# One-token attention with a gated MLP: where q is picked, how many key blocks TensorE scores, and the order of the last two tiles

## The chip, the cores and the metric

The kernel runs on one core of a Trainium2 chip. A core has a matrix engine (TensorE, PE in the profile), a vector engine (VectorE, DVE), a scalar engine (ScalarE, ACT), a general engine (GpSimd, POOL), and SyncE (SP), which here only issues DMA transfers. Sixteen DMA engines carry the transfers. The engines run side by side, each with its own list of instructions in order, and wait for each other by semaphores. The metric is the device time of one execution in microseconds (us); smaller is better.

## The reference

A gate mixes two branches that read the same token `x` of 512 values (everything is bfloat16):

```python
g = sigmoid((x * gate_w).sum(-1))
q = (x @ wq)                         # 32 heads of 128
scores = einsum("bhqd,bhkd->bhqk", q, k) * 128 ** -0.5    # 4096 keys per head
a = einsum("bhqk,bhkd->bhqd", softmax(scores), v) @ wo    # back to 512
h = relu(x @ w1 + b1)                # 1376 units
b = (h * h) @ w2 + b2
out = g * a + (1 - g) * b
```

The caches `k` and `v` have 32 heads x 4096 keys x 128 values, 33.5 MB each; `wq` and `wo` have 4.2 MB each, `w1` and `w2` 1.4 MB each. Each head has its own keys and values, and there is one query row, so every cached value is used once.

## The kernel before

**Tiles.** The attention goes over `NQ = 8` tiles of four heads. A tile of K is 128 partitions x 128 blocks x 128 values: partition `p` holds 128 consecutive keys of head `p // 32`, and a "block" is one key of every partition. A tile of K or V is one transfer of 4.19 MB. Three buffers hold K and two hold V; the last two V tiles are put in K's buffers.

**Scores in three ways.** The 128 blocks of a tile are divided:

- GpSimd multiplies four groups of `GB[i]` blocks by q (L308, into two buffers `pg`); VectorE sums each group over the 128 values (`psums`, L680).
- VectorE multiplies two groups of `XH[i]` blocks by q (`prods`, L665, q read from PSUM as `pQ`) and sums them (`sums`, L674).
- TensorE takes the rest in `NC[i]` chunks of eight blocks: it transposes each block (`transposes`, L428), ScalarE copies a chunk out of PSUM (`evac`, L336), and TensorE multiplies it by q (`scores`, L442); ScalarE copies the scores to `Sb` (`score_copy`, L342).

Before the change `NC` is 4 for tiles 0 to 2 and 5 after; `GB` and `XH` follow as 17 and 14, or 16 and 12.

**Softmax and values.** VectorE takes the maximum of each partition (`smax`, L687); TensorE transposes it (`max_rows`, L452), VectorE takes the maximum per head (`gmax`, L691), TensorE sends it back to all partitions (`max_cols`, L456), ScalarE negates it (`neg_max`, L346) and does the exponentials (`exps`, L353). TensorE multiplies them with V (`pv`, L473), ScalarE copies the result to `pvf` (`pv_copy`, L359), and TensorE adds the four useful rows into `O` (`extract`, L482). This is done for tile `i-1` and `i-2` while the scores of tile `i` are made.

**The start.** TensorE makes a column form of `x`, which ScalarE copies to `xcol` and, spread over 128 columns, to `xb`. Then it multiplies `xb` by `wq` for one tile after the other (L413). Each result has q of four heads in four diagonal pieces, which are picked into `qb`: even tiles by ScalarE (L328), odd tiles by VectorE (L652). Three PSUM buffers `T` hold the results, so a result waits until the one three before was picked. Semaphores `s_qb` and `s_qd` count the picked pieces of the two engines.

**The MLP.** Its hidden row is made on TensorE after tile 0's scores (`mlp_h`), copied by ScalarE, turned into columns `H` (`mlp_c`), and VectorE makes `(1 - g) * relu(h) ** 2` as `hs` in six operations, three shapes of two each (`mlp`, L698 and L701). `mlp_out` multiplies by `w2`. All MLP weights lie in the third K buffer, so K of tile 2 is loaded only after `mlp_out` (`s_ml`, L248). VectorE makes `b2g = (1 - g) * b2` in tile 1 (L725).

**The order of the transfers.** SyncE issues nearly all of them, in a fixed order (L269 to L292): K 0, MLP weights, `b2`, the last rows of `w2` in eight small transfers, K 1, V 0, K 2, then V and K in turn, and `wo` in five parts by rows (`TS`). A K load waits until its buffer was read by TensorE, VectorE and GpSimd (`s_t`, `s_mu`, `s_pm`), a V load until the product with the tile two before is done (`s_pv`).

**The end.** After the last tile, VectorE scales `O` (L732) and TensorE regroups it into columns `o2` (L545). `attn_rows` goes over the parts of `wo` as they land: rows up to 20 as wide products into `pO` (L555), which ScalarE copies to `pvf` (L383) and `wide_rows` adds to `acc` (L570); the others straight into `acc` (L561). VectorE adds `b2g` (L737) and SyncE stores the result.

The order on TensorE and VectorE at the end of the last loop is written out by hand. For VectorE, inside the loop over tiles:

```python
psums(i, 1)
prods(i, 1)
if i + 1 < NQ:
    q_psum(i + 1)
if i == 0:
    mlp()
if i == 1:
    eng.wait_ge(s_bb, 16)
    eng.tensor_scalar(b2g[:, :], b2w[:, :], omg[:, 0:1], None, ALU.mult).then_inc(s_g, 1)
psums(i, 2)
sums(i, 1)
```

Of the kernel before, what the change touches and what calls it, by code (L numbers as in the profile page):

```python
# [5 lines left out]
def bass_gated_mix__gqa_block_cached__dense_activation_squared_relu__decode_kernel(  # L6
# [30 lines left out]
    FG = 9  # L37
# [14 lines left out]
    NC = [4 if i < 3 else 5 for i in range(NQ)]  # L52
# [18 lines left out]
    TS = [0, 8, 16, 24, 30, 32]  # L71
# [15 lines left out]
    with ctx:  # L87
# [88 lines left out]

        s_x = sem("s_x")
# [60 lines left out]
        with nc.Block() as block:  # L238

            @block.sync  # L240
            def _(eng):
# [33 lines left out]
                eng.dma_start(b2w[0:128:32, :], B_b2.rearrange("(j p) -> j p", p=128)).then_inc(s_bb, 16)  # L275
# [18 lines left out]
            @block.gpsimd  # L294
            def _(eng):
                eng.memset(ident[:, :], 0.0).then_inc(s_id, 1)
                eng.wait_ge(s_id, 1)
                eng.affine_select(out=ident[:, :], in_=ident[:, :], compare_op=ALU.not_equal, fill=1.0,
                                  base=0, pattern=[[-1, 128]], channel_multiplier=1).then_inc(s_id, 1)
                for i in range(NQ):  # L300
                    eng.wait_ge(s_k[i % NK], 16 * (i // NK + 1))
                    eng.wait_ge(s_qd if i % 2 else s_qb, 4 * (i // 2 + 1))
                    g = GB[i]
                    for k in range(GP):
                        n = GP * i + k
                        if n >= 2:
                            eng.wait_ge(s_ps, n - 1)
                        eng.tensor_tensor(pg[:, n % 2, 0:g, :], Kt[:, i % NK, k * g * 128:(k + 1) * g * 128]  # L308
                                          .rearrange("p (b d) -> p b d", b=g),
                                          qb[:, i:i + 1, :].broadcast_to([128, g, 128]), ALU.mult)\  # L310
                           .then_inc(s_pm, 1)

            @block.scalar
            def _(eng):
                eng.dma_start(xrow[:, :], A_x[0, :, :]).then_inc(s_x, 16)
                eng.dma_start(grow[:, :], gate_w.rearrange("(a n) -> a n", a=1)).then_inc(s_x, 16)
                eng.dma_start(b1r[:, :], B_b1.rearrange("(a n) -> a n", a=1)).then_inc(s_b, 16)
                eng.wait_ge(s_xc, 1)
                eng.activation(xcol[:, :], XC, ACT.Copy).then_inc(s_xf, 1)
# [4 lines left out]
                for j in range(0, NQ, 2):  # L324
                    eng.wait_ge(s_qr, j + 1)
                    for h in range(4):
                        a, b = HP * h, HP * h + HP
                        eng.activation(qb[a:b, j, :], T[j % NT][a:b, h * 128:(h + 1) * 128], ACT.Copy)\  # L328
                           .then_inc(s_qb, 1)
# [31 lines left out]
                for i in range(NQ + 1):  # L361
                    if i == NQ:
                        pv_copy(NQ - 3)
                    if i < NQ:
# [15 lines left out]
                pv_copy(NQ - 2)  # L380
                pv_copy(NQ - 1)
                eng.wait_ge(s_ww, 1)
                eng.activation(pvf[:, :], pO[0:112, :], ACT.Copy).then_inc(s_wc, 1)  # L383

            @block.tensor
            def _(eng):
# [8 lines left out]
                eng.wait_ge(s_xf, 2)  # L395
                eng.wait_ge(s_zp, 1)
                eng.matmul(Z, onesf[:, :], zp[:, :], start=True, stop=True).then_inc(s_z, 1)

                def q_wait(j):
                    eng.wait_ge(s_qd if j % 2 else s_qb, 4 * (j // 2 + 1))  # L400

                def q_columns(j):
                    q_wait(j)
# [3 lines left out]
                eng.wait_ge(s_xf, 2)  # L407
                eng.wait_ge(s_wq, 16)
                for j in range(NQ):
                    if j >= NT:  # L410
                        q_wait(j - NT)
# [106 lines left out]
                def mlp_x():  # L518
                    eng.wait_ge(s_hs, 3)
# [53 lines left out]
                for i in range(NQ):  # L573
# [21 lines left out]
                    if i >= 2:  # L595
                        pv(i - 2, NG // 2, NG)
                max_rows(NQ - 1)
                extract(NQ - 3)
                max_cols(NQ - 1)
                pv(NQ - 2, 0, NG)  # L600
# [12 lines left out]
            def _(eng):  # L613
# [11 lines left out]
                for p, q in ((0, 0), (32, 20)):  # L625
# [10 lines left out]
                                         ALU.add, zp[:, :]).then_inc(s_zp, 1)  # L636
                eng.wait_ge(s_ez, 1)
# [5 lines left out]
                eng.wait_ge(s_g, 3)  # L643
                def q_psum(i):
                    eng.wait_ge(s_qd if i % 2 else s_qb, 4 * (i // 2 + 1))
                    eng.tensor_copy(PQ[:, i % 4, :], qb[:, i, :]).then_inc(s_pq, 1)

                for j in range(1, NQ, 2):
# [45 lines left out]
                def mlp():  # L694
                    eng.wait_ge(s_h, 2)
                    parts = [(128, 0, FG), (FR, FG, FN), (QX, FN, FN + TX)]
                    for p, a, b in parts:
                        eng.tensor_scalar(hr[0:p, a:b], H[0:p, a:b], 0.0, None, ALU.max).then_inc(s_hv, 1)  # L698
                    eng.wait_ge(s_hv, 3)
                    for p, a, b in parts:  # L700
                        eng.scalar_tensor_tensor(out=hs[0:p, a:b], in0=hr[0:p, a:b], scalar=omg[0:p, 0:1],  # L701
                                                 in1=hr[0:p, a:b], op0=ALU.mult, op1=ALU.mult)\
                           .then_inc(s_hs, 1)

                for i in range(NQ + 1):
# [10 lines left out]
                    if i < NQ:  # L716
                        psums(i, 1)
                        prods(i, 1)
                        if i + 1 < NQ:
                            q_psum(i + 1)  # L720
                        if i == 0:
                            mlp()
                        if i == 1:
                            eng.wait_ge(s_bb, 16)
                            eng.tensor_scalar(b2g[:, :], b2w[:, :], omg[:, 0:1], None, ALU.mult).then_inc(s_g, 1)  # L725
                        psums(i, 2)
                        sums(i, 1)
                eng.wait_ge(s_den, 1)
                eng.reciprocal(rden[:, :], DEN).then_inc(s_rd, 1)
                eng.wait_ge(s_rd, 1)  # L730
# [3 lines left out]
                eng.tensor_copy(o2[:, :], T[1][:, 0:NH]).then_inc(s_o2, 1)  # L734
                eng.wait_ge(s_acc, 1)
# [31 lines left out]
```

## Time and profile before

| | us |
|---|---|
| three runs, median (lowest to highest) | 191.07 (190.68 to 191.09) |
| the profiled execution: time | 191.85 |
| its span | 189.6 |
| VectorE busy | 150.3 |
| GpSimd busy | 132.9 |
| TensorE products busy | 105.0 |
| ScalarE busy | 74.5 |
| bytes moved by DMA | 78.47 MB, mean 414 GB/s |

The profile shows one execution. Its span runs from the first to the last instruction; the device time has some 2.3 us more around it. All times below are from the start of the span. A row of a group gives the line, the engine, the operation, the tiles (written <- read) with their shapes, the count, the busy time and the mean of one. A row of a timeline has start, duration, and the instruction. A row of a window has the length, then busy time and count for PE, PE's weight loads, DVE, ACT and POOL, then the granted TensorE clock, the busy share of the 16 DMA engines and GB/s.

### The profile page before, as it was taken

Reading aid. Unit: us, or ns where it says so; the run is one execution under the profiler, and the core shown is the slowest. Engines: PE = TensorE matmul, PEld = TensorE weight load, DVE = VectorE, ACT = ScalarE, POOL = GpSimd, SP = SyncE. Lnnn points to the kernel's source line nnn. Section 1 sums busy time; section 2 is a strip of 40 time slices with the busy share of each in tenths; the row PEclk is TensorE's granted clock in tenths of the full one; section 3 lists DMA queues with packets and bytes.
Section 4 is the critical chain, followed back from the end, with each engine's and each line's share of the span. In section 5 each row is a group of like instructions: output and inputs, shape, how many; then the busy total and the mean of one; then the engine's idle time right before and its main releaser. Section 6 shows DMA issues by size and latency. Waiting matters only on the chain. (4 is left out here: it accounts for less than half of the span.)

```text
span 189.6 us, 2722 instructions
## 1 busy us (share of the span) xinstructions
PE 105.0 (55%) x1118; PEld 61.7 (33%) x1118; DVE 150.3 (79%) x134; ACT 74.5 (39%) x174; POOL 132.9 (70%) x38
## 2 busy tenths in 40 slices
PE   1129867748212705942952775396284767139755
PEld 0113343307112701631541444235141752023512
DVE  6102489699999999999999999999999999960010
ACT  2103464208240800880295078139505571405201
POOL 1000199949699459998999999999999999900000
PEclk9999998857655555695695588559657675855965
DMA  6999899999999999999999999999999999999991
GB/s 221 443 442 442 381 441 412 429 442 442 439 430 423 415 429 422 436 432 436 442 432 436 429 404 429 436 429 436 432 442 436 436 404 436 418 430 398 418 411 64
DMA packets 3841, 78.47 MB, mean 414 GB/s; under 512 B 484, under 2 KB 590, under 8 KB 887
## 3 DMA queue, kind: packets, MB, share of 16 engines
q1 hardware_dynamic: 3824, 78.32, 97.0%
q8 instruction: 8, 0.13, 0.3%
q14 instruction: 3, 0.02, 0.0%
q10 hardware_dynamic: 6, 0.00, 0.0%
HBM read 78.32 MB, written 0.00 MB: 413 GB/s over the span
## 5 line engine op out<-in xcount | busy, mean ns | idle before, releaser
L308 POOL TENSOR_TENSOR pg<-Kt,qb 128x2048 f32<-128x2048 bf16 (+1 forms) x32 | 132.2, 4160 | 32.6 <-DMA Kt<-in_A_k_cache_dram 21.4
L680 DVE TENSOR_REDUCE Sb<-pg 128x16 f32<-128x2048 f32 (+1 forms) x32 | 74.3, 2323 | 0.1
L336 ACT ACTIVATE kT<-T 128x1024 bf16<-128x1024 bf16 x37 | 35.3, 1034 | 9.2 <-PE T L428 9.0
L428 PE MATMUL T<-ident,Kt 128*128 128x128 bf16 x296 | 24.8, 249 | 10.5 <-DMA Kt<-in_A_k_cache_dram 10.5
L665 DVE TENSOR_TENSOR pr<-Kt,pQ 128x1536 f32<-128x1536 bf16 (+1 forms) x16 | 29.5, 1844 | 1.0
L674 DVE TENSOR_REDUCE Sb<-pr 128x12 f32<-128x1536 f32 (+1 forms) x16 | 29.4, 1838 | 0.0
L428 PEld LDWEIGHTS T<-ident,Kt 128*128 128x128 bf16 x296 | 21.2, 113 | 14.0 <-DMA Kt<-in_A_k_cache_dram 11.9
L346 ACT ACTIVATE nM<-pM 128x4 f32<-128x4 f32 x8 | 1.4, 173 | 57.8 <-PE pM L456 57.8
L473 PE MATMUL pO<-Vt,E 128*16 128x512 bf16 x192 | 22.9, 568 | 1.0 <-issue 1.0
L442 PE MATMUL pS<-qc,kT 128*128 128x4 bf16 x296 | 13.3, 167 | 14.4 <-ACT kT L336 14.0
L353 ACT ACTIVATE E<-Sb,nM 32x128 bf16<-32x128 f32 x32 | 18.7, 584 | 0.9
L452 PE MATMUL pM<-identf,mp 128*1 128x128 f32 x8 | 3.0, 372 | 28.5 <-DVE mp L687 28.5
L442 PEld LDWEIGHTS pS<-qc,kT 128*128 128x128 bf16 x296 | 10.6, 100 | 18.3 <-ACT kT L336 18.1
L482 PE MATMUL pX<-pvf,pick 112*32 112x128 f32 x64 | 13.6, 385 | 1.4 <-ACT pvf L359 1.4
L652 DVE CAST qb<-T 32x128 bf16<-32x128 f32 x16 | 4.6, 287 | 10.2 <-PE T L413 9.8
L413 PE MATMUL T<-Vt,kT 128*128 128x512 bf16 x32 | 10.2, 462 | 3.5 <-DMA Vt<-in_A_wq_dram 3.5
L482 PEld LDWEIGHTS pX<-pvf,pick 112*32 112x32 f32 x64 | 9.1, 153 | 5.4 <-ACT pvf L359 2.8
L452 PEld LDWEIGHTS pM<-identf,mp 128*1 128x1 f32 x8 | 0.6, 80 | 29.8 <-DVE mp L687 29.8
L473 PEld LDWEIGHTS pO<-Vt,E 128*16 128x16 bf16 x192 | 6.6, 108 | 7.9 <-issue 6.4
L456 PE MATMUL pM<-gm,onesf 1*128 1x4 f32 x16 | 4.5, 349 | 6.8 <-DVE gm L691 6.3
L328 ACT ACTIVATE qb<-T 32x128 bf16<-32x128 f32 x16 | 4.3, 268 | 10.0 <-PE T L413 9.7
L353 ACT ACTIVATION_READ_ACCUMULATOR E<-Sb,nM 32x1 f32 x32 | 8.2, 255 | 0.0
(81 smaller groups left out, 74.6 us busy)
## 6 DMA issues: line engine op xcount, KB each, us to landing
Kt<-in_A_k_cache_dram SPq DMA_DIRECT2D x8, 4096.0 KB, 27.3
Vt<-in_A_v_cache_dram SPq DMA_DIRECT2D x6, 4096.0 KB, 28.5
Vt<-in_A_wq_dram SPq DMA_DIRECT2D x1, 4096.0 KB, 12.4
Kt<-in_A_v_cache_dram SPq DMA_DIRECT2D x1, 4096.0 KB, 33.8
Kt<-in_A_v_cache_dram SPq DMA_DIRECT2D x1, 3072.0 KB, 24.7
Vt<-in_A_wo_dram SPq DMA_DIRECT2D x3, 1024.0 KB, 30.9
Kt<-in_B_w_dram SPq DMA_DIRECT2D x1, 1376.0 KB, 24.5
Kt<-in_B_w_dram SPq DMA_DIRECT2D x1, 1152.0 KB
```

The lines of the kernel that those rows point to most:

```text
L308: eng.tensor_tensor(pg[:, n % 2, 0:g, :], Kt[:, i % NK, k * g * 128:(k + 1) * g * 128] .rearrange("p (b d) -> p b d", b=g), qb[:, i:i + 1, ...
L336: eng.activation(kT[:, n % NR, :], T[n % NT][:, :].bitcast(bf16), ACT.Copy).then_inc(s_ev, 1)
L353: eng.activation(E[a:b, j % NE, :, h], Sb[a:b, j % NS, :], ACT.Exp, bias=nM[a:b, 4 * j + h:4 * j + h + 1], scale=SCALE, accum_out=RS[a:b, ...
L413: mm = eng.matmul(T[j % NT][:, :], xb[:, t, :], wq_sb[:, t, j * 512:(j + 1) * 512], start=(t == 0), stop=(t == 3))
L428: mm = eng.transpose(T[n % NT][:, :].bitcast(bf16)[:, y * 128:(y + 1) * 128], Kt[:, i % NK, w * 128:(w + 1) * 128], ident[:, :])
L442: mm = eng.matmul(S[:, c * TC + y, :], kT[:, n % NR, y * 128:(y + 1) * 128], qc[:, 4 * i:4 * i + 4], start=True, stop=True)
L473: mm = eng.matmul(pO[r:r + 16, :], E[:, i % NE, 4 * y:4 * y + 4, :], VT(i)[:, y * 512:(y + 1) * 512], start=(y < 4), stop=(y >= NG - 4))
L482: mm = eng.matmul(O, pick[0:112, b, 28 - 4 * i:60 - 4 * i], pvf[:, b * 128:(b + 1) * 128], start=False, stop=(i == NQ - 1 and b == 3), ski ...
L652: eng.tensor_copy(qb[a:b, j, :], T[j % NT][a:b, h * 128:(h + 1) * 128]).then_inc(s_qd, 1)
L665: eng.tensor_tensor(pr[:, 0:x, :], Kt[:, i % NK, a * 128:(a + x) * 128] .rearrange("p (b d) -> p b d", b=x), PQ[:, i % 4:i % 4 + 1, :].bro ...
L674: eng.tensor_reduce(Sb[:, i % NS, a:a + x], pr[:, 0:x, :], AX.X, ALU.add).then_inc(s_sd, 1)
L680: eng.tensor_reduce(Sb[:, i % NS, k * g:(k + 1) * g], pg[:, n % 2, 0:g, :], AX.X, ALU.add)\
```

## The change

- All tiles have `NC = 4`: 32 blocks on TensorE, four groups of 17 on GpSimd, two groups of 14 on VectorE.
- q of tiles 1, 3 and 5 is picked by VectorE, of tiles 0, 2, 4, 6 and 7 by ScalarE.
- `mlp` is two operations over the whole of `H`, placed after VectorE's third sums of GpSimd's products.
- `b2g` is made at the start, before q is picked; the transfer of `b2` goes from SyncE's queue to ScalarE's.
- `xcol` is copied by VectorE.
- TensorE does the extraction of tile 5 and the product of tile 6 with V ahead of the last tile's maximum; ScalarE copies the result of tile 6 ahead of the last negated maximum. VectorE does the copy of tile 7's result and the one after the wide products.
- `wo` comes in four parts: the first two are joined.

```diff
-    NC = [4 if i < 3 else 5 for i in range(NQ)]
+    NC = [4] * NQ
...
-    TS = [0, 8, 16, 24, 30, 32]
+    TS = [0, 16, 24, 30, 32]
...
+        QD = [1, 3, 5]
+        QA = [j for j in range(NQ) if j not in QD]
+
+        def wait_q(eng, j):
+            if j in QD:
+                eng.wait_ge(s_qd, 4 * (QD.index(j) + 1))
+            else:
+                eng.wait_ge(s_qb, 4 * (QA.index(j) + 1))
...
                 eng.wait_ge(s_wm, 2)
-                eng.dma_start(b2w[0:128:32, :], B_b2.rearrange("(j p) -> j p", p=128)).then_inc(s_bb, 16)
...
                 eng.dma_start(b1r[:, :], B_b1.rearrange("(a n) -> a n", a=1)).then_inc(s_b, 16)
+                eng.wait_ge(s_wm, 1)
+                eng.dma_start(b2w[0:128:32, :], B_b2.rearrange("(j p) -> j p", p=128)).then_inc(s_bb, 16)
                 eng.wait_ge(s_xc, 1)
-                eng.activation(xcol[:, :], XC, ACT.Copy).then_inc(s_xf, 1)
...
-                for j in range(0, NQ, 2):
+                for j in QA:
...
                     if i == NQ:
                         pv_copy(NQ - 3)
+                        pv_copy(NQ - 2)
...
-                pv_copy(NQ - 2)
-                pv_copy(NQ - 1)
-                eng.wait_ge(s_ww, 1)
-                eng.activation(pvf[:, :], pO[0:112, :], ACT.Copy).then_inc(s_wc, 1)
...
-                max_rows(NQ - 1)
                 extract(NQ - 3)
-                max_cols(NQ - 1)
                 pv(NQ - 2, 0, NG)
+                max_rows(NQ - 1)
+                max_cols(NQ - 1)
                 extract(NQ - 2)
...
+                eng.wait_ge(s_xc, 1)
+                eng.wait_ge(s_xf, 1)
+                eng.tensor_copy(xcol[:, :], XC).then_inc(s_zp, 1)
...
+                eng.wait_ge(s_bb, 16)
+                eng.tensor_scalar(b2g[:, :], b2w[:, :], omg[:, 0:1], None, ALU.mult).then_inc(s_g, 1)
...
-                for j in range(1, NQ, 2):
+                for j in QD:
...
-                    parts = [(128, 0, FG), (FR, FG, FN), (QX, FN, FN + TX)]
-                    for p, a, b in parts:
-                        eng.tensor_scalar(hr[0:p, a:b], H[0:p, a:b], 0.0, None, ALU.max).then_inc(s_hv, 1)
-                    eng.wait_ge(s_hv, 3)
-                    for p, a, b in parts:
-                        eng.scalar_tensor_tensor(out=hs[0:p, a:b], in0=hr[0:p, a:b], scalar=omg[0:p, 0:1],
-                                                 in1=hr[0:p, a:b], op0=ALU.mult, op1=ALU.mult)\
-                           .then_inc(s_hs, 1)
+                    eng.tensor_scalar(hr[:, :], H, 0.0, omg[:, 0:1], ALU.max, ALU.mult).then_inc(s_hv, 1)
+                    eng.wait_ge(s_hv, 1)
+                    eng.scalar_tensor_tensor(out=hs[:, :], in0=H, scalar=0.0, in1=hr[:, :], op0=ALU.max, op1=ALU.mult)\
+                       .then_inc(s_hs, 1)
...
+                        psums(i, 2)
                         if i == 0:
                             mlp()
-                        if i == 1:
-                            eng.wait_ge(s_bb, 16)
-                            eng.tensor_scalar(b2g[:, :], b2w[:, :], omg[:, 0:1], None, ALU.mult).then_inc(s_g, 1)
-                        psums(i, 2)
                         sums(i, 1)
...
+                eng.wait_ge(s_pv, NQ)
+                eng.tensor_copy(pvf[:, :], pO[0:112, :]).then_inc(s_pc, 1)
                 eng.wait_ge(s_rd, 1)
...
+                eng.wait_ge(s_ww, 1)
+                eng.tensor_copy(pvf[:, :], pO[0:112, :]).then_inc(s_wc, 1)
                 eng.wait_ge(s_acc, 1)
```

More of the change, by code (lines that the diff above doesn't have):

```diff
@@ L301, in _ @@
                     eng.wait_ge(s_k[i % NK], 16 * (i // NK + 1))
-                    eng.wait_ge(s_qd if i % 2 else s_qb, 4 * (i // 2 + 1))
+                    wait_q(eng, i)
                     g = GB[i]
@@ L394, in _ @@
                 mm.then_inc(s_xc, 1)
-                eng.wait_ge(s_xf, 2)
-                eng.wait_ge(s_zp, 1)
+                eng.wait_ge(s_xf, 1)
+                eng.wait_ge(s_zp, 2)
                 eng.matmul(Z, onesf[:, :], zp[:, :], start=True, stop=True).then_inc(s_z, 1)
-                def q_wait(j):
-                    eng.wait_ge(s_qd if j % 2 else s_qb, 4 * (j // 2 + 1))
                 def q_columns(j):
-                    q_wait(j)
+                    wait_q(eng, j)
                     eng.transpose(QT[:, j, :], qb[:, j, :], ident[:, :]).then_inc(s_qt, 1)
-                eng.wait_ge(s_xf, 2)
                 eng.wait_ge(s_wq, 16)
@@ L410, in _ @@
                     if j >= NT:
-                        q_wait(j - NT)
+                        wait_q(eng, j - NT)
                     for t in range(4):
@@ L518, in mlp_x @@
                 def mlp_x():
-                    eng.wait_ge(s_hs, 3)
+                    eng.wait_ge(s_hs, 1)
                     eng.matmul(HX, selh[:, :], hs[0:QX, FN:FN + TX], start=True, stop=True).then_inc(s_hx, 1)
@@ L596, in _ @@
                         pv(i - 2, NG // 2, NG)
+                extract(NQ - 3)
+                pv(NQ - 2, 0, NG)
                 max_rows(NQ - 1)
-                extract(NQ - 3)
                 max_cols(NQ - 1)
-                pv(NQ - 2, 0, NG)
                 extract(NQ - 2)
@@ L636, in _ @@
                                          ALU.add, zp[:, :]).then_inc(s_zp, 1)
+                eng.wait_ge(s_xc, 1)
+                eng.wait_ge(s_xf, 1)
+                eng.tensor_copy(xcol[:, :], XC).then_inc(s_zp, 1)
                 eng.wait_ge(s_ez, 1)
@@ L643, in _ @@
                 eng.wait_ge(s_g, 3)
+                eng.wait_ge(s_bb, 16)
+                eng.tensor_scalar(b2g[:, :], b2w[:, :], omg[:, 0:1], None, ALU.mult).then_inc(s_g, 1)
                 def q_psum(i):
-                    eng.wait_ge(s_qd if i % 2 else s_qb, 4 * (i // 2 + 1))
+                    wait_q(eng, i)
                     eng.tensor_copy(PQ[:, i % 4, :], qb[:, i, :]).then_inc(s_pq, 1)
-                for j in range(1, NQ, 2):
+                for j in QD:
                     eng.wait_ge(s_qr, j + 1)
```

## The prediction

> **What bounds the kernel now.** I read the forty slices and the queues first. No slice of the DMA row between the first and the last is below 8, so I then asked for the stretches as windows.
>
> ```profile
> DMA  6999899999999999999999999999999999999991
> q1 hardware_dynamic: 3824, 78.32, 97.0%
> q8 instruction: 8, 0.13, 0.3%
> ```
>
> ```profile
> 32.00:172.00 140.00, 76.12 (x840) 48.33 (x842) 133.74 (x91) 59.26 (x135) 123.07 (x30) 0.66 1.00 430
> 172.00:184.00 12.00, 9.10 (x102) 4.13 (x94) 0.74 (x3) 3.52 (x10) 0.00 (x0) 0.78 0.98 408
> 184.00:187.20 3.20, 2.27 (x56) 1.13 (x60) 0.00 (x0) 0.60 (x1) 0.00 (x0) 0.50 0.48 193
> ```
>
> The last two columns are the busy share of the 16 DMA engines and GB/s: 1.00 and 430 for 140 us. VectorE is busy 133.74 us in the same stretch, but the transfers never stop for it. The third line has a share of 0.48: the engines do not finish together. The trace's landing records put the sixteen completions of the last wo transfer between 184.94 and 187.11, mean 186.07; the slowest engine sets the time. That last landing is also the issue of the fifth wo transfer (152.71) plus its time to landing:
>
> ```profile
> Vt<-in_A_wo_dram SPq DMA_DIRECT2D x1, 256.0 KB, 34.4
> ```
>
> The chain that ended last says the same, and adds a second thread beside it:
>
> ```profile
> 151.75 32.87 DMA Vt<-in_A_wo_dram
> ...
> 184.66 0.62 PE pO L555 x3
> ...
> 185.31 0.61 ACT pvf L383
> ...
> 185.96 0.61 PE pX L570 x8
> 186.56 1.01 PE pX L561 x24
> ...
> 187.59 0.29 DVE b2w L737
> ```
>
> After wo's third transfer lands (184.62), four wide products, ScalarE's copy, the reduction at L570 and the rows at L561 follow. The last eight rows start at 187.15, when both the earlier rows are through and the last transfer has landed (187.11). So the end is a tie of the last landing and this thread, then 2.4 us to the span's end that nothing here touches.
>
> Are the transfers ever about to run out? SyncE's timeline gives the issues:
>
> ```profile
> 42.87 0.80 SPq L249 DMA_DIRECT2D Kt<-in_A_k_cache_dram  x2
> ...
> 78.04 0.33 SPq L258 DMA_DIRECT2D Vt<-in_A_v_cache_dram  x1
> ...
> 149.95 0.80 SPq L267 DMA_DIRECT2D Kt<-in_A_v_cache_dram  x2
> ```
>
> By 42.87, 19.6 MB had been issued (wq, two K, one V of 4.19 MB, MLP weights 2.8) and 17.15 moved: 2.45 MB left, 5.7 us at 430. At 78.04: 36.37 issued, 32.26 moved, 9.5 us left. At 149.95: 69.93 and 63.14, 15.8 us left. Every other issue has at least 12 us. An issue may come that much later, or any amount earlier, and the queue does not notice.
>
> **The change part by part.**
>
> *32 TensorE blocks in every tile.* Tiles 3 to 7 go from 16 and 12 blocks a group to 17 and 14. The rows for both sizes exist: GpSimd 4.308 against 4.072 us, VectorE's sums 2.407 against 2.272, its products and sums 2.012 and 2.004 against 1.743 and 1.738. VectorE's time for one tile is read from its timeline:
>
> ```profile
> 66.38 2.02 DVE L665 TENSOR_TENSOR pr<-Kt,pQ 128x1792 f32<-128x1792 bf16 x1
> ...
> 84.38 1.75 DVE L665 TENSOR_TENSOR pr<-Kt,pQ 128x1536 f32<-128x1536 bf16 x1
> ...
> 100.91 1.75 DVE L665 TENSOR_TENSOR pr<-Kt,pQ 128x1536 f32<-128x1536 bf16 x1
> ```
>
> 18.0 us for tile 2 (large), 16.5 for tile 3 (small), 16.4 after. A pair of tiles' worth of DMA is 8.39 MB, 19.5 us, so 18.0 still fits under it. Cost on VectorE 5 x 1.6 = 8.0 us. TensorE and ScalarE lose 40 transposes, 40 score products and five evictions of 1.03 us, off the path.
>
> *VectorE's early stalls go.* These two rows are the ones to remove:
>
> ```profile
> 38.31 1.97 DVE L701 SCALAR_TENSOR_TENSOR hs<-hr,omg 128x9 bf16<-128x9 f32 x3
> ...
> 58.21 3.79 DVE L725 TENSOR_SCALAR b2g<-b2w,omg 128x128 f32<-128x128 bf16 x1
> ```
>
> Both end with one of GpSimd's products (39.99, 61.91). b2g moves ahead of GpSimd's first product (22.90), where a 128x128 cast takes 0.28. The units become two operations; with H in PSUM each has one SBUF operand, like L665, which runs beside GpSimd. I take 0.2 each (L701's small forms, 0.21), bounded above by the blocked 1.71. Placed after the third sums they run at about 38.4 instead of waiting for H until 37.98. Moving q 7 to ScalarE lets the first products start at 23.1, when K lands, not 25.51. In sum tile 1 starts at about 40.9 (was 44.66). Then a new limit: K of tile 2 lands at 60.49 whatever VectorE does, so tile 2 starts there (was 66.38), 5.9 us earlier. Five tiles of 18.0 put tile 7 at 150.5 (was 150.11), and the last maximum at 171.0 (was 168.96): 2.0 us later.
>
> *Tile 6 ahead of the last maximum.* Before, extraction and 32 products of tile 6 lay behind that maximum; now they fill 167.4 (V lands) to 170.9. After the maximum: transpose, VectorE's maximum, broadcast, exps of 2.4 us, ready at 175.0. Tile 7's first 24 products end near 176.6, the rest wait for V's last part (149.95 + 0.4 + 26.8 = 177.15) and end about 178.2 (was 178.73). With VectorE's copy, extraction (1.06), oT and regrouping the rows of wo can start at about 181.1; they started at 181.61. Before as after, they are ready ahead of the weights.
>
> *wo in four transfers.* The first 16 rows are one transfer, landing near 182.1, where 8 landed at 179.65. Sixteen wide products took 1.76 us in pieces, so they end by 183.9, ahead of 184.6: hidden, 0.7 us to spare. 16 packets of 8 KB per DMA engine become 8 of 16 KB. In the packet records 8 KB takes 312 ns, 24 KB 915, so 16 KB about 613: 8 x (624 - 613) = 0.09 us sooner. One transfer less also saves each engine a completion of 9 ns. The Trainium skill's "DMA: Bandwidth & Descriptors", section Bandwidth, gives about 3 cycles of fixed cost a packet; at its 850 MHz that would be an estimate of 0.03 us for 8 packets; the trace's own packets say three times that.
>
> *The copy behind the wide products moves from ScalarE to VectorE.* ScalarE takes 0.597. VectorE has no 112x512 copy from PSUM. Below: its memset of 128x512, 0.485. Above: the rate of its PSUM-fed products, 1.743 for 1536, gives 0.74 for 512 with the 0.16 of a small operation. Nearest: casts from PSUM, 0.192 for 32 columns and 0.287 for 128, extended to 512: 0.67. I take 0.67: +0.07 on the thread, ends -0.11 and +0.14.
>
> *Start-up.* b2's transfer goes to ScalarE's queue, and VectorE now waits for it ahead of its q casts, with GpSimd's first operand, TensorE's q products and SyncE's K of tile 2 behind it in the end. On that queue the row of b1, issued at 1.52, landed at 10.6, the gate at 8.06; one more place puts b2 at 11 to 15, against 16.95 when the first cast is due. Bounds: nothing, or, if it queued as on SyncE where it landed at 29.8, 13 us. I take nothing. xcol's copy goes to VectorE, about 0.2 us before ez; wq lands only at 13.13, so it hides. SyncE's queue gives K of tile 1 0.64 us earlier, into 10 us of backlog: nothing.
>
> *Sum.* Last landing 187.11 - 0.10 = 187.01. Thread: third transfer 184.62 - 0.10, then 2.53 as before, + 0.07 = 187.12 for the last eight rows (was 187.15). Change -0.03 on 191.85, the profiled execution (span 189.59 and 2.26 around it): 191.82. That execution is 0.78 above the median of 191.07; applied there, 191.04, so 191.0. About 0.2%, 0.38 us, is what a measurement of this kernel tells from no change.
>
> **The rivals.**
>
> *Faster: the slowest DMA engine sheds load.* At 49.94 the sixteen landings of V spread over 1.55 us, at 60.49 over 2.39, and the spread stays. Between lie instruction fetches (50.5, 53.0, 58.9): one engine, already behind from the eight small transfers of w2's last rows, took 0.84 more. TensorE loses 160 of its 2236 instructions, all later than that, but VectorE and ScalarE fetch at other points. If that fetch falls on another engine the next in line ends 0.5 earlier: 190.5. For it: fetches after 80 us do hit engines with slack. Against it: the tail thread, at 187.12, caps the gain unless wo's third transfer is earlier by as much, which it is when the same engine is relieved. The Trainium skill's "Runtime: NRT & Kernel Launch", section Instruction fetch mechanics, has blocks of 256 instructions fetched while the engine runs, at a cost mostly hidden; the 16 KB packets agree on the size.
>
> *Slower by the same lottery.* Another fetch falls on that engine: +0.6, 191.65.
>
> *Slower: VectorE's heavier tiles reach the end.* Rows of wo must be started by 182.7 to end before the third transfer; I have 181.1, so 1.6 us to spare. If a tile takes 18.5, not 18.0, five make 2.5, and 0.9 shows: 192.0. Against it: tile 2 did take 18.0, with no wait.
>
> *Slower: b2 lands late.* It decides when it lands after about 23.6 (16.95 + 5.7 of backlog + about 1 gained by the units). At 29.8 K of tile 2 would find a dry queue for 6 us: 197. Against it: b1's 10.6.
>
> **How the numbers follow.** Unchanged end 0.52 (190.7 to 191.4); lighter engine 0.26 (190.2 to 190.7); heavier engine 0.08, VectorE late 0.08, b2 late 0.06. Faster 0.26, same 0.52, slower 0.22. The range reaches to both fetch cases and to VectorE's, 190.3 to 192.0, and leaves out b2.
>
> **What would show it.** Right: DMA share 1.00 throughout; wo's last landing near 187.0; tile 2's products at 60.5 and tile 7's at 150.5; rows of wo waiting for their transfers. Wrong: a slice of DMA below 8; VectorE's b2g after 17; wo's rows starting after 182.7; a last landing at 186.6 or 187.7.

## The result, and the profile after

The changed kernel takes 190.62 us (median of 21 runs, 190.41 to 191.18) against 190.88 us for the kernel before (21 runs beside it, 190.57 to 192.27): a ratio of 0.9979, 95% interval 0.9969 to 0.9989 (ratios here are those on record; plain means of the runs give 0.9980, the two medians 0.9986). That is 0.21% or about 0.4 us less by the ratio and 0.26 us by the medians, at the edge of the 0.2% that the prediction named as the limit of this measurement. The forecast was 191.0 us, no measurable change. The measured 190.62 lies in its range (190.3 to 192.0), but not in the 190.7 to 191.4 of its likeliest case: it falls into the 190.2 to 190.7 to which it gave a chance of 0.26.

The profiled execution after took 190.65 us with a span of 189.2, against 191.85 and 189.6 before. Of the 1.2 us between them only 0.4 lie inside the span; the rest is the time around the span, which was 2.26 us in that execution of the kernel before and 1.45 here. Over all recorded runs the span averages 189.18 us in the changed kernel (21 runs) and 189.41 in the kernel before (77 runs beside the experiments): 0.23 us are gained inside the span. The time around it is 1.41 to 1.53 us in the changed kernel; in the kernel before its median is 1.50, but some runs have up to 3.2. All that follows is about what lies inside the span.

The forty slices and the queue of instructions of the changed kernel's page:

```profile
DMA  6999999999999999999999999999999999999991
q8 instruction: 8, 0.13, 0.3%
```

Two of the same stretches as windows (length, then busy time and count for PE, weight loads, VectorE, ScalarE, GpSimd, then the granted TensorE clock, the DMA engines' busy share and GB/s):

```profile
32.00:172.00 140.00, 78.62 (x790) 50.12 (x788) 135.83 (x86) 55.03 (x129) 127.98 (x30) 0.60 1.00 430
184.00:187.20 3.20, 2.72 (x64) 1.18 (x60) 0.69 (x1) 0.00 (x0) 0.00 (x0) 0.57 0.43 166
```

No slice of the DMA row between the first and the last is below 9, and the 140 us in the middle again have a share of 1.00 at 430 GB/s. VectorE and GpSimd do more work than before (135.83 us against 133.74, 127.98 against 123.07) and the transfers do not notice. The chain that ended last, from the issue of wo on:

```profile
150.61 33.73 DMA Vt<-in_A_wo_dram
...
184.39 0.62 PE pO L558 x4
...
185.04 0.70 DVE pvf L740
...
185.78 0.60 PE pX L573 x8
186.39 0.80 PE pX L564 x32
...
187.21 0.29 DVE b2w L743
```

It is the same chain as before, with VectorE's copy in the place of ScalarE's. Its first link, the landing of the third last part of wo, comes at 184.34 instead of 184.62, and its rows end at 187.18 instead of 187.57. Of this 0.39 us, 0.28 lie in when wo lands. The other 0.1 lies between the last landing and the end of the rows (0.35 us instead of 0.46), at a granted clock of 0.57 instead of 0.50 in the window from 184.0 to 187.2. The trace's landing records give sixteen completions for each transfer, one for each DMA engine:

| us | before | after |
|---|---|---|
| first completion of wo's last part | 184.94 | 184.83 |
| mean of the sixteen | 186.07 | 185.85 |
| last completion | 187.11 | 186.83 |

The mean came 0.22 us earlier. The prediction had 0.10 for it.

### The profile page after: what moved, and what is told of

It is laid out like the page before. It is cut to its first block, busy times and chain, and to the rows that moved or that the text cites. A ratio compares the mean times of both kernels' runs of the same rounds, so it can differ in the third digit from the quotient of the medians.

```text
span 189.2 us, 2552 instructions
## 1 busy us (share of the span) xinstructions
PE 107.2 (57%) x1038; PEld 63.5 (34%) x1038; DVE 153.4 (81%) x129; ACT 69.6 (37%) x170; POOL 137.8 (73%) x38
## 5 line engine op out<-in xcount | busy, mean ns | idle before, releaser
L317 POOL TENSOR_TENSOR pg<-Kt,qb 128x2176 f32<-128x2176 bf16 x32 | 137.1, 4319 | 28.6 <-ACT qb L338 21.4
L689 DVE TENSOR_REDUCE Sb<-pg 128x17 f32<-128x2176 f32 x32 | 76.9, 2405 | 2.4 <-POOL pg L317 2.4
L346 ACT ACTIVATE kT<-T 128x1024 bf16<-128x1024 bf16 x32 | 30.8, 1030 | 17.9 <-PE T L431 17.8
L674 DVE TENSOR_TENSOR pr<-Kt,pQ 128x1792 f32<-128x1792 bf16 x16 | 32.2, 2011 | 1.9 <-DMA Kt<-in_A_k_cache_dram 1.1
L683 DVE TENSOR_REDUCE Sb<-pr 128x14 f32<-128x1792 f32 x16 | 32.1, 2003 | 0.0
L431 PEld LDWEIGHTS T<-ident,Kt 128*128 128x128 bf16 x256 | 22.7, 132 | 23.8 <-DMA Kt<-in_A_k_cache_dram 22.5
L445 PE MATMUL pS<-qc,kT 128*128 128x4 bf16 x256 | 11.7, 167 | 9.8 <-ACT kT L346 9.6
L485 PE MATMUL pX<-pvf,pick 112*32 112x128 f32 x64 | 15.3, 421 | 2.4 <-ACT pvf L369 1.6
L476 PE MATMUL pO<-Kt,E 128*16 128x512 bf16 x64 | 7.2, 627 | 2.0 <-issue 2.0
L661 DVE CAST qb<-T 32x128 bf16<-32x128 f32 x12 | 3.4, 287 | 5.9 <-PE T L416 5.7
```

The source lines that it names most:

```text
L346: eng.activation(kT[:, n % NR, :], T[n % NT][:, :].bitcast(bf16), ACT.Copy).then_inc(s_ev, 1)
L431: mm = eng.transpose(T[n % NT][:, :].bitcast(bf16)[:, y * 128:(y + 1) * 128], Kt[:, i % NK, w * 128:(w + 1) * 128], ident[:, :])
L445: mm = eng.matmul(S[:, c * TC + y, :], kT[:, n % NR, y * 128:(y + 1) * 128], qc[:, 4 * i:4 * i + 4], start=True, stop=True)
L476: mm = eng.matmul(pO[r:r + 16, :], E[:, i % NE, 4 * y:4 * y + 4, :], VT(i)[:, y * 512:(y + 1) * 512], start=(y < 4), stop=(y >= NG - 4))
L485: mm = eng.matmul(O, pick[0:112, b, 28 - 4 * i:60 - 4 * i], pvf[:, b * 128:(b + 1) * 128], start=False, stop=(i == NQ - 1 and b == 3), ski ...
L674: eng.tensor_tensor(pr[:, 0:x, :], Kt[:, i % NK, a * 128:(a + x) * 128] .rearrange("p (b d) -> p b d", b=x), PQ[:, i % 4:i % 4 + 1, :].bro ...
```

## Where the steps of the prediction stood in the trace after

The early part came as worked out. VectorE's timeline of the changed kernel (start, duration, instruction, then idle time before it and its releaser):

```profile
12.78 0.29 DVE L651 TENSOR_SCALAR b2g<-b2w,omg 128x128 f32<-128x128 bf16 x1 [2.35 <-DMA b2w<-in_B_b_dram]
...
38.65 0.23 DVE L705 TENSOR_SCALAR hr<-pX,omg 128x13 f32<-128x13 f32 x1 [0.29 <-PE pX L518]
38.92 0.17 DVE L707 SCALAR_TENSOR_TENSOR hs<-pX,hr 128x13 bf16<-128x13 f32 x1
...
41.15 2.02 DVE L674 TENSOR_TENSOR pr<-Kt,pQ 128x1792 f32<-128x1792 bf16 x1
...
59.91 2.02 DVE L674 TENSOR_TENSOR pr<-Kt,pQ 128x1792 f32<-128x1792 bf16 x1 [0.90 <-DMA Kt<-in_A_k_cache_dram]
...
149.91 2.02 DVE L674 TENSOR_TENSOR pr<-Kt,pQ 128x1792 f32<-128x1792 bf16 x1
...
170.00 0.28 DVE L696 TENSOR_REDUCE mp<-Sb 128x1 f32<-128x128 f32 x1
```

b2 landed at 12.7 (11 to 15 forecast) and its scaling took 0.29 where the blocked one had taken 3.79; the two MLP operations took 0.23 and 0.17 (0.2 each forecast). Tile 1 starts at 41.15 (40.9), tile 2 at 59.91 when its K lands (60.5), tile 7 at 149.91 (150.5), and the last maximum is at 170.00 (171.0).

The end of TensorE's work did not come as worked out. TensorE's timeline:

```profile
175.01 3.59 PE L476 MATMUL pO<-Kt,E 128*16 128x512 bf16 x32
179.40 1.91 PE L485 MATMUL pX<-pvf,pick 112*32 112x128 f32 x8 [0.79 <-DVE pvf L733]
...
182.44 2.54 PE L558 MATMUL pO<-Vt,o 128*1 128x512 bf16 x20 [0.28 <-DVE o L738]
```

The rows of wo start at 182.44; the prediction had 181.1, and before they started at 181.61. Tile 7's products could start earlier than before, but 32 of them took 3.59 us where 29 had taken 1.89, and the extraction 1.91 instead of 1.06. In these windows the granted clock is 0.50 in the changed kernel and was 1.00 in the kernel before. Changed kernel:

```profile
176.00:180.00 4.00, 3.21 (x31) 1.14 (x20) 0.69 (x1) 0.00 (x0) 0.00 (x0) 0.50 1.00 424
```

Kernel before:

```profile
176.00:180.00 4.00, 3.29 (x47) 2.41 (x47) 0.15 (x1) 0.60 (x1) 0.00 (x0) 1.00 1.01 422
```

It cost nothing: the sixteen products of wo's first part fit in before the third last part, the second of four, lands at 184.34. The clock of 0.50 belongs to this one execution, not to the new order: in the changed kernel with wo in five transfers (below), whose order is the same, the granted clock was 1.00 from 180 to 184 us, the extraction took 1.06 us and the rows started at 181.71.

## The experiments

**The theory after the result.** A: the transfers run without a pause from 32 us on, and the DMA engine that finishes last sets the end. Whatever takes DMA time out of the stream moves the landing by a sixteenth of it on the mean. Two parts of the change do so: eight 16 KB packets per engine in the place of sixteen of 8 KB (wo's first two parts joined), and fewer instructions that TensorE has to fetch over the same engines. The edits at the start of VectorE's list and the order at the end are worth nothing in themselves, but make room for the smaller number of TensorE blocks. B, the rival: the gain comes from an earlier start of the last tiles or from the new order at the end, and the DMA records are by the way.

How the fetches are seen: the queue of instructions shows packets of 16 KB, 1.02 to 1.12 us long each. Eight of them start before wo's last landing in the kernel before (30.9, 50.5, 80.7, 97.9, 113.7, 133.2, 152.4, 173.6 us), and seven in the changed kernel (31.0, 50.4, 73.9, 95.5, 116.0, 137.9, 161.9), with the eighth at 184.25 when the stream is nearly over. As each of these fifteen ends, one packet begins that is about half a us longer than its like: 32 KB in 1.68 to 1.76 us instead of 1.21, and behind the one at 173.6, 8 KB in 0.86 us instead of 0.31. TensorE has 160 instructions fewer, 2 x 1,038 against 2 x 1,118.

### wo's parts joined, alone and left out

The kernel before with this edit only, and the changed kernel with the edit undone:

```diff
-    TS = [0, 8, 16, 24, 30, 32]
+    TS = [0, 16, 24, 30, 32]
```

> The kernel before with one edit: wo comes in four transfers instead of five. Theory A (the end is set by the slowest DMA engine's queue, and the computation is hidden): 8 packets of 16 KB replace 16 of 8 KB on each engine, so -0.05 to -0.1 us against the kernel before, ratio 0.9995, within its interval of 1. Theory B (the gain of 0.26 us came from the computation, by VectorE's stalls or the order of the last tiles): 0, or slower, since 16 rows now wait for one landing. Theory C (the whole gain came from wo's transfers): -0.26 us or more, ratio 0.998.

Measured: 190.97 against 191.03 us, ratio 1.0000 (0.9984 to 1.0017).

> The changed kernel with wo in five transfers again. Theory A: +0.05 to +0.1 us against the changed kernel, so about -0.2 us against the kernel before (ratio 0.999). Theory B: the whole gain stays, ratio 0.998. Theory C: the gain is gone, ratio 1.000.

Measured: 190.74 us, ratio 0.9984 (0.9969 to 0.9998). The times alone do not tell these kernels from their neighbours. The landing records do: alone, the edit brings the mean landing from 186.07 to 186.01, the last from 187.11 to 187.04; undone in the changed kernel, the mean goes from 185.85 to 185.96 and the last from 186.83 to 187.01. That is 0.06 and 0.11 us (0.09 and 0.08 when each trace is counted from an early landing, in the table below), and a 16 KB packet takes 0.615 us (0.613 was interpolated).

### 32 blocks on TensorE, alone and left out

The kernel before with this edit only, and the changed kernel with it undone:

```diff
-    NC = [4 if i < 3 else 5 for i in range(NQ)]
+    NC = [4] * NQ
```

> The kernel before with one edit: 32 blocks on TensorE in every tile, without the other parts. VectorE starts tile 7 five times 1.6 us later, 158.1, and the last maximum comes at 178.6 instead of 169.0 (five tiles and the rest of tile 7: +9.6). The rows of wo start 9.6 us later, 191.2, and the slack there is about 1 us. Both theories: about +8.5 us, 199.5 (197 to 201); transfers never run dry, since the fewest us in the queue at an issue is 5.7 at 42.87, before tile 3. If it stays below 192, VectorE has slack that the timeline does not show.

Measured: 196.81 us, ratio 1.0282 (1.0248 to 1.0317); the profiled execution took 195.22. VectorE's and TensorE's timelines of this kernel:

```profile
156.45 2.02 DVE L665 TENSOR_TENSOR pr<-Kt,pQ 128x1792 f32<-128x1792 bf16 x1
```

```profile
188.93 1.25 PE L555 MATMUL pO<-Vt,o 128*1 128x512 bf16 x20 [0.28 <-DVE o L734]
```

Without the edits at the start VectorE is late at the end: tile 7 starts at 156.45 (150.11 in the kernel before), and the rows of wo at 188.93, 2.1 us after wo's last landing at 186.81. VectorE has become the bound. My 199.5 was too large because five tiles of 1.6 us were counted ahead of tile 7's start, where four lie (tiles 3 to 6: 6.4, measured 6.34). The landing itself is earlier here too: mean 185.94 against 186.07.

> The changed kernel with the old division of the blocks (five chunks on TensorE in tiles 3 to 7, groups of 16 and 12). VectorE then does five tiles in 16.4 us instead of 18.0, so 8 us less work. Theory A (the end is the last landing of the slowest DMA engine): no gain, 190.6 plus or minus 0.25 (TensorE has 160 instructions more to fetch). K of tile 7 lands at 147.8 and stops VectorE there. Theory B (VectorE's tiles are on the path): faster by more than 0.5 us, below 190.1.

Measured: 191.06 against 191.08 us, ratio 1.0002 (0.9987 to 1.0017). With all the rest of the change kept and the old number of blocks, the gain in time is gone. Only a part of that loss is inside the span: it averages 189.28 us here, 189.18 in the changed kernel and 189.47 in the kernel before beside it. The rest is time around the span (1.72 us or more in every run here, 1.41 to 1.53 in the changed kernel), which no experiment explains. VectorE's timeline of this kernel:

```profile
128.36 1.75 DVE L674 TENSOR_TENSOR pr<-Kt,pQ 128x1536 f32<-128x1536 bf16 x1 [1.09 <-DMA Kt<-in_A_k_cache_dram]
...
147.77 1.75 DVE L674 TENSOR_TENSOR pr<-Kt,pQ 128x1536 f32<-128x1536 bf16 x1 [3.15 <-DMA Kt<-in_A_k_cache_dram]
...
166.39 0.28 DVE L696 TENSOR_REDUCE mp<-Sb 128x1 f32<-128x128 f32 x1
```

VectorE now waits for K (1.09 and 3.15 us), and its last maximum is 3.6 us earlier than in the changed kernel. That bought nothing, which speaks against B. Its mean landing is 186.00 against 185.85, a difference of 0.15 us here and 0.13 in the run before. The last landing of this profiled execution, 186.84, does not differ from the changed kernel's 186.83, so the step from the mean to the last engine is one of chance in a single trace.

These differences come from one trace for each kernel, and the traces differ already when K 1 lands, near 39 us, long before tile 3 and wo. Counted from that landing, they tell far more:

| mean of sixteen landings, us | K 1 | wo's last part | between |
|---|---|---|---|
| kernel before | 39.29 | 186.07 | 146.79 |
| kernel before, wo joined | 39.32 | 186.01 | 146.70 |
| kernel before, 32 blocks | 39.25 | 185.94 | 146.69 |
| changed kernel | 39.23 | 185.85 | 146.62 |
| changed, wo in five transfers | 39.26 | 185.96 | 146.70 |
| changed, old number of blocks | 39.28 | 186.00 | 146.71 |
| changed, old order of the last tiles | 39.18 | 185.80 | 146.62 |

The last row, an experiment below, leaves the transfers as they are and shows how little the last column scatters; the three below with other small transfers of `w2`, all ahead of K 1, have 146.61 to 146.63. So wo joined is worth 0.09 and 0.08 us, the blocks 0.10 and 0.09, and the two add up to the 0.17 of the change. The old number of blocks with all the rest of the change (146.71) is where wo alone brings the kernel before (146.70): the edits at the start and the new order do not show in the transfers after K 1. The other 0.06 of the 0.22 lie ahead of K 1's landing. Whether the edits at the start bring them, or only chance, was not tested.

### The order of the last tiles undone

The changed kernel, with `max_rows` of tile 7 ahead of tile 5's extraction again, `max_cols` ahead of tile 6's products, and ScalarE's copy of tile 6 after the last exponentials:

```diff
-                extract(NQ - 3)
-                pv(NQ - 2, 0, NG)
                 max_rows(NQ - 1)
+                extract(NQ - 3)
                 max_cols(NQ - 1)
+                pv(NQ - 2, 0, NG)
                 extract(NQ - 2)
```

> The changed kernel with the last tiles' order undone: the last maximum goes first to TensorE, then the extraction of tile 5, the broadcast, and the products of tile 6; ScalarE copies tile 6's result after the last exps. Products of tile 6 (3.6 us at the granted clock of 0.50), its copy and extraction (1.9) come behind the maximum again. Rows of wo start at about 186.9 instead of 182.4, against a slack of about 1 us: +3.5 to +4.5 us, 194.1 to 195.1. If the order hides nothing: 190.6.

Measured: 190.72 us, ratio 0.9982 (0.9966 to 0.9999). A miss by more than 3 us. TensorE's timeline and the end of the chain of this kernel:

```profile
173.04 3.59 PE L476 MATMUL pO<-Kt,E 128*16 128x512 bf16 x32
...
178.29 1.89 PE L476 MATMUL pO<-Kt,E 128*16 128x512 bf16 x29
180.99 1.06 PE L485 MATMUL pX<-pvf,pick 112*32 112x128 f32 x8 [0.81 <-DVE pvf L733]
```

```profile
183.16 2.09 PE pO L558 x20
...
185.27 0.70 DVE pvf L740
...
187.29 0.29 DVE b2w L743
```

I had counted tile 6's products and extraction as 3.6 us and more in front of the rows of wo. They lie beside the exponentials of tile 7 (173.35 to 175.8), for which TensorE waits anyway, and tile 7's products and extraction then ran at a granted clock of 0.92 (window 176 to 180) in 1.89 and 1.06 us instead of 3.59 and 1.91 at 0.50. So the rows of wo start 0.72 later, at 183.16, and VectorE's copy 0.23 later. In this execution wo's third last part landed at 184.18, but its chain runs through the rows from 183.16 on and not through that landing: with the old order the rows of wo set the end, if only by a little. The new order is worth 0.1 us at the end of the chain, which the time does not show.

### b2's transfer back on SyncE's queue

```diff
                 eng.wait_ge(s_wm, 2)
+                eng.dma_start(b2w[0:128:32, :], B_b2.rearrange("(j p) -> j p", p=128)).then_inc(s_bb, 16)
```

(taken out of ScalarE's list; VectorE still waits for b2 ahead of its q)

> The changed kernel with b2's transfer back on SyncE's queue, where it landed at 29.8 in the kernel before, while VectorE still makes b2g ahead of its q casts. VectorE waits 17 us; the q casts, tile 0's sums, the MLP and K of tile 2 (issued at 41.7, queue dry at about 48.6) come 10 us later. Theory A: the DMA engines run dry for 3 to 4 us, and the end comes 3 to 6 us later, 194 to 197, with a slice of the DMA row below 8 near 50. If nothing waits for it in the end: 190.6.

Measured: ratio 1.062 (1.0566 to 1.0674), which rests on two executions of 201.77 (the profiled one) and 204.12 us. VectorE's and SyncE's timelines and the page:

```profile
29.84 1.65 DVE L650 TENSOR_SCALAR b2g<-b2w,omg 128x128 f32<-128x128 bf16 x1 [19.38 <-DMA b2w<-in_B_b_dram]
```

```profile
56.51 0.80 SPq L259 DMA_DIRECT2D Kt<-in_A_k_cache_dram  x2
```

```profile
DMA  7999899995059999999999999999999999999980
```

This is the rival in which b2 lands late, made to happen. K of tile 2 is issued at 56.51 instead of 41.69, the tenths of the DMA row fall to 5, 0 and 5, and K of tile 2 lands at 68.87 instead of 59.89: 14.8 us of delay less 9.0 shown leaves 5.8 us that the backlog covered, against the 5.7 of the prediction. The size of the rival was too small: 6 us of dry queue were forecast and 9 came, since the delay was not 13 us but 14.8 (the scaling, now beside GpSimd again, took 1.65 instead of 0.29), and the 1 us from the earlier units, which I had counted as a further margin, is already in the 41.69. The last landing, 196.55, moved by 9.7 and the span by 11.0: here the chain at the end goes through tile 7's exponentials and products, and the rows of wo start only at 195.30. Why the other execution took 2.4 us more stays open.

### The five slowest DMA engines: loaded more, and relieved

The last 40 rows of `w2` come in eight transfers of five rows. After them the landings of K 1 in the changed kernel show five engines 0.96 to 1.28 us behind the first, a sixth that a fetch had just hit at 1.63, and ten within 0.58. The first edit issues these eight transfers twice, the second copy to a part of the buffer that nothing uses:

```diff
+                for r in range(4):
+                    for p, q in ((0, 0), (32, 20)):
+                        eng.dma_start(spare[p + r:p + 20:4, :], w2_x[q + r:q + 20:4, :]).then_inc(s_w2, 16)
                 load_k(1)
```

> The changed kernel with the suspected cost doubled: the eight transfers of 5 rows are issued a second time, into an unused part of the same buffer (0.12 MB more). Theory A: the five DMA engines that carry them fall 1.2 us further behind, and the end with them: +1.2 us against the changed kernel, 191.8, ratio to the kernel before 1.005. If the 16 engines shared the load evenly: 0.12 MB at 430 GB/s is 0.3 us, 190.9. Theory B (the computation sets the end): 190.6.

Measured: 192.10 us, ratio 1.0053 (1.0035 to 1.0071). The copy is 0.12 MB, 0.3 us of the whole stream. The mean landing came 0.40 later, the last 1.08 later (187.91), and the time is 1.5 us above the changed kernel's 190.62. So the end follows the engine that finishes last and not the mean. The Trainium skill's page "DMA: Bandwidth & Descriptors", section "Why a DMA increments its semaphore by 16 and not by 1", lets such a transfer use the largest number of engines up to 16 that divides its rows, here five, and always the lowest-numbered ones. The five late engines agree with the number; which engines they are, the landing records do not tell.

The next edit puts the same 40 rows into two transfers of 20 rows each:

```diff
-                for r in range(4):
-                    for p, q in ((0, 0), (32, 20)):
-                        eng.dma_start(WX[p + r:p + 20:4, :], w2_x[q + r:q + 20:4, :]).then_inc(s_w2, 16)
+                for p, q in ((0, 0), (32, 20)):
+                    eng.dma_start(WX[p:p + 20, :], w2_x[q:q + 20, :]).then_inc(s_w2, 16)
```

> The changed kernel with w2's last 40 rows in two transfers of 20 rows instead of eight of 5 rows. The packet records show the eight of 5 rows on the same five DMA engines, 8 packets of 3 KB each, 1.2 us behind the others from then on; two of 20 rows should go over ten engines with 4 packets each. Theory A: the slowest engine gets 0.6 us back, but five others lose 0.6, so the last landing moves by -0.6 (the slowest engine stays alone) to 0 (another engine that had instruction fetches takes its place); I expect 190.3, ratio to the kernel before 0.9965. Theory B: nothing changes, 190.6.

Measured: 191.14 us, ratio 1.0006 (0.9989 to 1.0024): 0.5 slower than the changed kernel where a gain was expected. The forty packets of 3 KB took 7.85 us in all instead of 6.05, and the sixteen first packets of K 1, which run beside them, 1.43 to 2.03 us, where eleven had taken 1.35 to 1.50 in the changed kernel (elsewhere 1.21). The rows lie on neighbouring partitions here and four apart before, so I tried a version that spreads them over every third partition, in transfers of 32 and 8 rows:

```diff
+                for a, b in ((0, 32), (32, 40)):
+                    eng.dma_start(WX[3 * a:3 * b - 2:3, :], w2_x[a:b, :]).then_inc(s_w2, 16)
```

> The changed kernel, with the last 40 rows of w2 loaded by two transfers of 32 and 8 rows, every third partition (0, 3, ... 117), instead of eight transfers of 5 rows that all go through the same five DMA engines. Bytes are the same. Theory A (the DMA engine that finishes last sets the end, and the eight 5-row transfers make five engines the last): these five get back about 5 packets of 3 KB, some 0.15 us each by the issue page of the run with 20-row transfers, 0.75 us, and the others take 0.3 to 0.45 more; the last landing of wo comes 0.2 to 0.5 us earlier than the changed kernel's 186.83 and the time is 190.1 to 190.4, ratio 0.996 to 0.997. Theory B (the mean over the engines sets the end): nothing moves, 190.6, ratio 0.998. The price of the run with 20-row transfers on neighbouring partitions (slower by 0.5 us) would come again only if two large transfers are dear whatever partitions they go to: then 191.1.

Measured: 190.96 us against 190.90, ratio 0.9991 (0.9970 to 1.0011), 0.3 us above the changed kernel's median. The interval of this ratio and that of the changed kernel overlap, but the mean span, 189.47 against 189.18, and the landings agree that it is slower. Also a miss, and an instructive one. At K 1's landing fifteen engines are within 0.58 us, so the five were relieved as expected. But the mean landing of K 1 is 0.20 us later (39.43 against 39.23): all sixteen first packets of K 1 took 1.37 to 1.71 us, where eleven had taken 1.35 to 1.50 in the changed kernel. The excess of K 1's packets over 1.213 us adds up to 6.55 us instead of 4.06, and the 3 KB packets to 6.56 instead of 6.05; these 3.0 us over 16 engines are the 0.19 that the mean lost. In nine traces with the eight small transfers unchanged these three numbers scatter (39.17 to 39.32, 3.03 to 4.75, 5.47 to 6.28); both variants lie outside. And the last landing of wo, 187.13, is again 2.1 us behind the first, as in the changed kernel (2.0): by then the fetches have made other engines the last ones. Which packets contend for what (neighbouring partitions, or only how many engines read the small rows at once) is not told apart by these two runs.

### TensorE's instructions alone

If the fetches count, more instructions must cost, even where TensorE has time to spare. The changed kernel with 64 products of one element by one element in each tile, written to a column that nothing reads:

```diff
+                    for _ in range(64):
+                        eng.matmul(pM[0:1, 400:401], ident[0:1, 0:1], ident[0:1, 0:1], start=True, stop=True)
```

> The changed kernel, with 64 products of one element by one element added to each of the eight tiles on TensorE, into a column that nothing reads: 1,024 more instructions of TensorE, 64 KB, which are four more packets of 16 KB on the queue of instructions. VectorE and the transfers are not changed. Theory A (every 16 KB of TensorE's instructions that are fetched while the stream runs shift one DMA engine by about 1.5 us, as the landings showed, which is 0.09 us on the mean of 16): the mean landing of wo's last transfer comes 0.35 to 0.4 us later, the last landing 0.3 to 0.6, time 191.0 to 191.2, ratio 1.000 to 1.001. Theory B (the number of TensorE's instructions is hidden; the gain of the change came from elsewhere): 190.6, ratio 0.998.

Measured: 191.75 us, ratio 1.0039 (1.0020 to 1.0058), 1.1 us above the changed kernel. Two lines of this kernel's page, and the first link at the end of its chain:

```profile
q8 instruction: 12, 0.20, 0.4%
L591 PE MATMUL pM<-ident 1*1 1x1 bf16 x512 | 13.9, 158 | 0.0
```

```profile
150.99 34.19 DMA Vt<-in_A_wo_dram
```

Four packets of 16 KB more, as intended, and the chain is the same one with a later landing. The mean landing is 186.17 against 185.85, later by 0.32 (0.35 to 0.4 expected), the last 187.66 against 186.83, later by 0.83 (0.3 to 0.6 expected). Counted from K 1's landing the mean is 0.35 later (146.97 against 146.62). The time is half a microsecond above the 191.0 to 191.2 that were expected. In the landings each fetch can be followed: between 138 and 149 us one engine's offset to the first jumps from about 1.5 to 3.0 us, by 158 us a second, by 168 a third. As far as the offsets tell, each is an engine that had been hit once before. So a fetch costs its engine about 1.5 us, not the 0.61 us that 16 KB take in the stream. Its own packet takes about 1.06 us, and the packet of 32 KB behind it, as at 32.0 us in the changed kernel, 1.72 instead of 1.21. Sixteenths of 1.5 us for four fetches are 0.37 us; 0.35 was measured from K 1's landing on.

The Trainium skill's page "Runtime: NRT & Kernel Launch", section "Instruction fetch mechanics", calls the cost of crossing a 16 KiB boundary "mostly hidden". For TensorE's own progress nothing in these runs speaks against it; for a kernel whose end is set by the DMA engines, this run measures a price.

## Why the prediction was right, and where it was not

**The bound was read rightly.** DMA share 1.00 throughout, the end set by the DMA engine that finishes last, then the thread through the wide products: the chain after and the doubled small transfers show both.

**wo in four parts, -0.10: right.** The runs have -0.08 and -0.09 on the mean landing, counted from K 1's.

**VectorE's copy, +0.07: right.** It took 0.69 us (0.67 taken), ScalarE's 0.60. It lies on the thread, and the earlier landing of wo's third last part (184.34, forecast 184.52) more than paid for it.

**32 blocks on TensorE, off the path: the step that failed.** The prediction says of the 40 transposes and 40 score products that they are "off the path", and enters nothing for them in the sum. On TensorE that is so. But the 160 instructions have to be fetched, over the DMA engines that bound the kernel. The prediction named the 160 instructions only in a rival on where fetches fall, as a matter of luck, not as less DMA time. The term that was left out is -0.09 to -0.10 us on the mean landing, counted from K 1's, shown by adding the edit to the kernel before, by taking it from the changed kernel, and, from the other side, by 1,024 added instructions (+0.35 for four fetches). One fetch fewer before the last landing explains all of it: 1.5/16 = 0.09. With -0.09 in the sum the last landing would have been 186.92 (measured 186.83), the last eight rows 187.03 instead of 187.12, and the forecast 190.95; what is still missing is of the size of the 0.06 ahead of K 1's landing and of the scatter of the last engine.

**Its cost on VectorE, 8.0 us hidden by the early stalls: right, and shown to be needed.** Without the edits at the start the same tiles cost 5.7 us.

**Tile 6 ahead of the last maximum: right that it buys next to nothing, with less room than said.** The prediction had the rows of wo ready at 181.1, ahead of the weights before as after. In the profiled execution tile 7's products ran at a granted clock of 0.50 and the rows started at 182.44, 0.26 us short of the 182.7 beyond which the prediction would have seen them in the time. That was near the condition of the rival of a late VectorE, though by way of TensorE's clock and not of VectorE, whose last maximum was 1.0 us earlier than forecast. With the old order the rows started at 183.16 and lay on the chain at the end.

**b2 on ScalarE's queue, nothing: right.** It landed at 12.7, ahead of the first cast at 16.55. On SyncE's queue it costs some 6% (1.062 against 0.9979).

**The rival that came nearest** is the lighter slowest engine, 190.5 with a chance of 26%. Its place was wrong in part: what was measured is not one fetch falling on another engine, but the whole mean moving by 0.22, with the spread between first and last engine shrinking from 2.17 to 2.00. What the rival described did happen for one transfer: at K of tile 2 the spread was 1.85 instead of 2.39 us, but at the next landing, near 70 us, it was 2.29 again. That a time in this rival's interval came out is luck as far as its mechanism goes.

## What to carry to other kernels

When the DMA engines are busy from end to end, every byte on them counts, the instructions too: count the instructions that an edit removes or adds on each engine, and price a 16 KB fetch by what the landings show, not by its bytes. When two traces are compared, count their landings from an early one that the edit can't have moved: here K 1's own mean landing scatters over 0.15 us in nine traces, and the stretch behind it over 0.02 in five that have the same transfers there. Look at the landings of single engines and not only at their mean, because small transfers with few rows load the same few engines each time, and the last engine sets the end. An edit that is worth nothing in itself (here the early stalls on VectorE) can be what makes another one affordable, so try a part alone and left out before it is called useless.

## What the runs showed of the hardware that was not expected

- A fetch of 16 KB of instructions sets one DMA engine back by about 1.5 us in a saturated stream: about 1.06 us for itself, and 0.5 more on the packet behind it (1.68 to 1.76 us where 32 KB take 1.21). Four fetches more moved the mean of sixteen engines by 0.35 us, one fewer by 0.09 to 0.10.
- Forty packets of 3 KB took 6.05, 6.56 or 7.85 us in all, depending on how their rows were spread over transfers and partitions, and the packets of K 1 beside them took 4.06, 6.55 or 9.84 us more in all than at 1.213 us each. Fewer and better balanced transfers were slower.
- TensorE's granted clock between 180 and 184 us was 0.50 in the profiled execution of the changed kernel, and 0.70 to 1.00 in six others with the same order of the last tiles (wo in five transfers, the old number of blocks, the three with other transfers of `w2`, the added instructions). The eight products of the extraction took 1.91 us in the first and 1.06 in all the others. What decides it was not tested.
